# Two steps of VectorE in a kernel of attention and feed-forward: sums of weights put in front of a row's adds, the scaling of x put into the next row

## The chip, the cores and the metric

The kernel runs on one core of a Trainium2 chip. Its time is the device time in microseconds (us), and the number for a kernel is the median of its runs. One execution is taken by the hardware profiler as well; times inside the kernel are from that execution, counted from its first instruction.

The engines are TensorE (PE in the profile; PEld is its loading of weights), VectorE (DVE), ScalarE (ACT), GpSimd (POOL) and SyncE (SP). Each works through its own queue, and semaphores hold an instruction until what it needs is there.

## The reference

Attention for 4 batches of 8 heads, with 768 positions of 64 numbers, and on its result a feed-forward block:

```python
q_bits = (np.einsum('bhsd,dk->bhsk', q, proj) > 0)     # 6 bits: a bucket
mask = q_bucket[:, :, :, None] == k_bucket[:, :, None, :]
scores = np.where(mask, scale * np.matmul(q, k.transpose(0, 1, 3, 2)), -1e9)
attn = softmax(scores)
x = np.matmul(attn, v)        # (B,H,S,D) -> (3072 tokens, 512)
...
g = x @ w_gate                # 512 -> 1536
return (silu(g) * (x @ w_val)) @ w_out
```

All of it is in 32-bit floats.

## The kernel before, in words

**Rows.** The 8 heads of a batch are taken two by two, so there are 16 pairs, numbered n = 0 to 15, four to a batch. Each pair is done in two rows, one for each half of its 768 queries; half 0 comes first. A row has six chunks of 128 keys. The loop at L843 writes one row after the other. For each chunk, `score` (L484) makes the products of q and k for two heads and adds the products of the hash bits into the same bank of PSUM; ScalarE takes the exponential of them into a tile A (L497). `add` (L518) lets VectorE add up the chunks into a tile acc, five instructions (L523, then L527 four times). `attend` (L500) then multiplies A with v (PSUM tile av), and ScalarE copies the result to xT (L516).

**The sums of the softmax.** After the half-1 row's `attend`, `total` (L529) sums acc over its partitions on TensorE (four products into the tile sum, L540), VectorE takes the reciprocal (L548), and eight DMAs of SP spread it over the partitions (L553). The scaling of x is `norm` (L558): one VectorE instruction at L560 multiplies xT of both halves by the spread reciprocals. `total` doesn't write it out but puts it into the list `waiting`, and the main loop decides when the list is emptied (`finish(waiting)`).

**The feed-forward block of a batch** is cut into atoms, which the rows of the next batch take from the list `atoms` behind their attention; a row takes atoms of size 14 (15.75 from pair 8 on), which is one group, or sometimes two. The last batch's atoms run after the last row, one behind the other (L914). Per batch there are six up groups, which make the gate and value products, and then three chunks of the output product (`down_strassen`, tile po). Both use Strassen's scheme: seven products of sums of blocks instead of eight products of blocks. The sums of x are put into the list `first` and written out before the first group.

**An up group** (`both`, L618) is ten atoms in the batches whose scheme is nested (`nested`, all but the first batch). Each atom has one outer product (`outer`, L651), which TensorE makes as fp32 products of 128x384. Two of the outer products, numbered d = 0 and d = 1, are again split into seven products of 128x192 (`deeper`, L694): those are the inner products. They need four sums of weight blocks, which `weigh(d)` (L687) makes on VectorE, 128x128 each, into the tile inner for d = 0 and words for d = 1 (the fourth into the weights' own place in room). Before the change, weigh(0) is written out in atom 1, in front of atom 2, which has the first inner products. All matmuls are written by `product` (L581) and all plain sums by `plus` (L587), so that the profile has them under L584 and L588. After each inner product its bank of PSUM is added into a tile c or hid (L588); three inner products that add into the same bank each have to wait until the one before has been read. At the end of a group `settle` writes out what is left of the gates: L571 multiplies by 1 + tanh, where the tanh is ScalarE's L570, and L575 multiplies gate and value.

**Weights** come by DMAs of GpSimd (`bring`, L322) from DRAM into two places, for every group anew. Each place is filled in three parts, and a part is fetched as soon as the products that used it are done (`free`, L645). Weigh(0) uses the block A12, which is a part by itself.

**Which row has what.** From pair 8 on, a batch's eight rows take: output chunk and up group 0 (half 0); groups 1 to 5, one in each row; then two output chunks, the second in a half-1 row. With pair 8 that is: group 1 in 8's half-1 row, 2 and 3 in pair 9, 4 and 5 in pair 10, output chunks in pair 11, and pair 12 begins with a chunk and the next batch's group 0. So the half-1 rows of pairs 8, 9, 10, 12, 13 and 14 have an up group, and the half-0 rows of pairs 9, 10, 13 and 14.

**The order of the work is written out by hand**: each engine's queue has its instructions in the order in which the program writes them. Before the change the list `waiting` is emptied inside a row's atoms, once atoms of size 11 have been written (L899), so that the scaling of pair n stands in the half-1 row of n, near the end of the group:

```python
            if part >= 11 or u + NCH == N and part >= 6:
                finish(waiting)
```

and weigh(0) stands in the group that uses it:

```python
                    todo[at - 1].insert(0, lambda at, d=d: weigh(d))
```

Of the kernel before, what the change touches and what calls it, by code (L numbers as in the profile page):

```python
# [18 lines left out]
def kernel(  # L19
# [16 lines left out]
    NCH = S // P  # L36
# [3 lines left out]
    NP = H // 2  # L40
# [260 lines left out]
    def scale_ahead():  # L301
        scale_to(min(progress["piece"] + 4, progress["scaled"] + 1))
# [82 lines left out]
    atoms = []  # L385
# [92 lines left out]
    LATE = NP * 2 * NCH  # L478
# [5 lines left out]
    def score(u):  # L484
        n, half, c = units[u]
        qs = slice(half * HQ, (half + 1) * HQ)
        ks = slice(c * P, (c + 1) * P)
        sc = [bank("sc")[:, 0:HQ] for _ in range(2)]
        for x, start in ((T, True), (bits, False)):
            if u < 2 and not start:  # L490
                prepare_pair(1)
            for h in range(2):
                rows = slice(h * D, (h + 1) * D)
                nc.tensor.matmul(sc[h], x["k", n][rows, ks], x["q", n][rows, qs],  # L494
                                 start=start, stop=not start)
        for h in range(2):
            nc.scalar.activation(weights(u)[:, h, 0:HQ], sc[h], AF.Exp,  # L497
                                 scale=SCALE * (OFF / 2 if n <= NP else 1.0))
# [79 lines left out]
    def gate_tile():  # L578
        return ffn.tile([P, HQ], FP32, tag="c", name="c", bufs=5)

    def product(ps, pairs_, start):  # L581

        for i, (a, x) in enumerate(pairs_):
            nc.tensor.matmul(ps, a, x, start=start and i == 0, stop=i == len(pairs_) - 1,  # L584
                             skip_group_check=True)

    def plus(o, a, b, op=ALU.add):  # L587
        nc.vector.tensor_tensor(o, a, b, op=op)  # L588

    def up_strassen(x, b, first):  # L590
# [14 lines left out]
        nested = b > 0  # L605
# [12 lines left out]
        def both(i):  # L618
# [15 lines left out]
            def settle(at):  # L634
                while later and later[0][0] <= at:
                    later.pop(0)[1]()
# [14 lines left out]
            def outer(n, g, at):  # L651
                my = now[g]
                block, to, xs = (
                    (A11, "a", [x[j][:, lo] for j in range(2)]),
                    (S1, "b", [x[j][:, hi] for j in range(2)]),
                    (S2, "a", [t2[:, j] for j in range(2)]),
                    (A12, "c", [x[2 + j][:, lo] for j in range(2)]),
                    (S3, "a", [t3[:, j] for j in range(2)]),
                    (S4, "b", [x[2 + j][:, hi] for j in range(2)]),
                    (A22, "a", [t4[:, j] for j in range(2)]),  # L660
                )[n]
                w = places[g][:, block, :].rearrange("p (j m) -> p j m", m=P)
                if to not in my:
                    my[to] = bank("up")[:, 0:HQ]
                c = my[to]
                product(c, [(w[:, j], xs[j]) for j in range(2)], n in (0, 1, 3))
                spot = ((0, 0), (1, 1), (0, 1), (0, 0), (1, 1), (0, 1), (1, 0))[n]
                copies = (0, 2, 4) if nested else (0, 1, 2)
                if n in copies:
                    nc.scalar.copy(tile_of(g, spot), c)  # L670
                    if n == 4:
                        nc.scalar.copy(tile_of(g, (1, 0)), c)
                elif n < 6:
                    plus(my[spot], my[spot], c)
                    c = my[spot]
                settle(at)
                if n not in copies:
                    finished(g, spot, c, at, 1 if n == 6 else 2)
                free(g, n)
# [3 lines left out]
            def inner_weights(block, rs):  # L683
                vs = [places[g][:, block, j * P : (j + 1) * P] for g in range(2) for j in range(2)]
                return (*vs, *(rs[:, k] for k in range(3)), vs[2])

            def weigh(d):  # L687
                _, block, *_, rs, _ = deep[d]
                v11, v12, v21, v22, r1, r2, r3, r4 = inner_weights(block, rs)
                for o, p, q, op in ((r3, v11, v21, ALU.subtract), (r2, v22, r3, ALU.subtract),  # L690
                                    (r1, r2, v11, ALU.add), (r4, v12, r2, ALU.subtract)):
                    plus(o, p, q, op)
# [29 lines left out]
            todo = [[lambda at, n=n, g=g: outer(n, g, at)] for n in order for g in range(2)]  # L722
            if nested:
                for d, at in ((0, 2), (1, 6)):
                    for go in range(4):
                        todo[at + go].insert(0, lambda at, d=d, go=go: deeper(d, go, at))
                    todo[at - 1].insert(0, lambda at, d=d: weigh(d))

            def step(at):
                if at == 0:  # L730
                    while first:
                        first.pop(0)()
                for do in todo[at]:
                    do(at)
                if at == len(todo) - 1:
                    settle(at + NB)

            for at in range(len(todo)):
                size = 2 if nested and at in (2, 3, 6, 7) else 1
                atoms.append((size, lambda at=at: step(at), at == len(todo) - 1))  # L740

        for i in range(NG // 2):
            both(i)
# [87 lines left out]
    def prepare_pair(count):  # L831
        for _ in range(count):
            rest.extend(f for f in steps.pop(0)() or [] if f)

    def finish(todo):
        while todo:
            todo.pop(0)()

    prepare_pair(4)
    finish(rest)  # L840
    N = len(units)
    credit = 0.0
    for u in range(0, N, NCH):  # L843
        n, half, _ = units[u]
        gating = u >= LATE
        if u == MOVE:
            progress["late"] = True
            for t in late_ring:
                nc.gpsimd.memset(t[:, :, HQ:AW], 1.0)
        for c in range(NCH):  # L850
            score(u + c)
            if u + c == 2 or not gating and half == 1 and c == 2:
                prepare_pair(1)
            if c == 1 and half == 0 and 0 < n <= NP:
                total(n - 1)
            if c:
                add(u + c)
        if half == 1 and n < NP or u == LATE:
            finish(waiting)
        finish(rest)  # L860
        if not gating and half == 0:
            steps = front(n + 1)
        if not gating and half == 0 and u > 0:
            prepare_pair(2)
        for _ in range(1 if u else 2):
            scale_ahead()
        for c in range(NCH):
            attend(u + c)
        if not gating:
            scale_ahead()  # L870
        if half == 1:
            load(n + 2, "qkv" if n + 2 > NP else "v")
        elif not gating:
            prepare_pair(2 if u > 0 else 4)
            if n + 2 <= NP:
                load(n + 2, "qk")
        finish(first)
        prepare_on(0 if u == LATE else 4)
        chores = []
        if half == 1 and n >= NP:  # L880
            total(n)
            if n + 1 < len(pairs):
                chores = [None] + steps.pop(0)()
        prepare_on(0 if LATE - NCH <= u <= LATE else 3 if gating or not half else 1)
        if not gating:
            continue
        if n + 1 < len(pairs) and half == 0:
            steps = front(n + 1)
            chores = [None, steps.pop(0), None, steps.pop(0)]

        credit += 14 if n < 2 * NP else 15.75
        end = True
        part = 0
        while atoms and (credit > 0 or not end):
            size, atom, end = atoms.pop(0)
            credit -= size
            atom()
            part += size
            if part >= 11 or u + NCH == N and part >= 6:  # L899
                finish(waiting)  # L900
                if u + NCH == N:
                    finish([first.pop(0) for _ in range(min(2, len(first)))])
            if 5 < part < 14 if u == LATE else part < (9 if u < LATE + 3 * NCH else 11):
                prepare_on(size)
            if 6 < part < 11 or u == LATE and part > 10:
                scale_ahead()
            for _ in range(size):
                if chores:
                    step = chores.pop(0)
                    chores.extend(step and step() or [])  # L910
        while chores:
            step = chores.pop(0)
            chores.extend(step and step() or [])
# [34 lines left out]
```

The softmax here doesn't subtract the row's maximum and nothing guards it: scores larger than these inputs give would overflow.

## Time and profile before

| | us |
|---|---|
| median of 3 runs | 999.0 (998.54 to 999.03) |
| span of the profiled execution | 997.5 |
| TensorE busy in it | 980.5 (98%) |
| VectorE busy | 671.7 (67%) |
| ScalarE busy | 407.7 (41%) |

The profile is read in this order: the busy time by engine; who waited for whom (a line has engine and source line, the releaser, the total in us, the number of times and the longest); the windows, which give for a stretch of time its length and each engine's busy time in it; and the timeline, in which each line has the start, the length, the engine, the line of the kernel, the operation, the tiles written and read, and how many such instructions are drawn together. An fp32 product is two passes in the profile, so that 34 products of a group are 68 entries.

The chain of work that ended last is nearly all TensorE:

```profile
PE 90%; DVE 6%; issue 2%; ACT 2%; POOL 0%; DMA 0%; DVEq 0%; ACTq 0%; POOLq 0%
```

### The profile page before, as it was taken

Reading aid. Unit: us, or ns where it says so; the run is one execution under the profiler, and the core shown is the slowest. Engines: PE = TensorE matmul, PEld = TensorE weight load, DVE = VectorE, ACT = ScalarE, POOL = GpSimd, SP = SyncE. Lnnn points to the kernel's source line nnn. Section 1 sums busy time; section 2 is a strip of 40 time slices with the busy share of each in tenths; the row PEclk is TensorE's granted clock in tenths of the full one; section 3 lists DMA queues with packets and bytes.
Section 4 is the critical chain, followed back from the end, with each engine's and each line's share of the span. In section 5 each row is a group of like instructions: output and inputs, shape, how many; then the busy total and the mean of one; then the engine's idle time right before and its main releaser. Section 6 shows DMA issues by size and latency. Waiting matters only on the chain.

```text
span 997.5 us, 13575 instructions
## 1 busy us (share of the span) xinstructions
PE 980.5 (98%) x4813; PEld 624.5 (63%) x4813; DVE 671.7 (67%) x1276; ACT 407.7 (41%) x921; POOL 126.9 (13%) x248
## 2 busy tenths in 40 slices
PE   9999999999999999999999999999999999999998
PEld 4444555555577765655566775665656786666687
DVE  5898988888965556777783456776776446667631
ACT  6999555565512233444432313443452202232200
POOL 3222232231100011011010001111110001121000
PEclk9999999999999999999999999999999999999999
DMA  7777685876313043333322114343131102233001
GB/s 233 223 243 227 164 260 174 226 268 154 103 29 75 17 116 92 90 98 78 100 79 58 51 32 111 93 106 92 58 92 33 34 31 90 74 116 101 5 29 36
DMA packets 119987, 107.02 MB, mean 107 GB/s; under 512 B 90032, under 2 KB 104848, under 8 KB 119920
## 3 DMA queue, kind: packets, MB, share of 16 engines
q0 software_dynamic: 18336, 73.29, 22.6%
q1 hardware_dynamic: 100784, 32.67, 14.0%
q8 instruction: 38, 0.62, 0.3%
q10 hardware_dynamic: 800, 0.20, 0.1%
q14 instruction: 29, 0.24, 0.1%
HBM read 81.79 MB, written 17.30 MB: 99 GB/s over the span
## 4 chain that ended last, share of the span: by engine, by line
PE 90%; DVE 6%; issue 2%; ACT 2%; POOL 0%; DMA 0%; DVEq 0%; ACTq 0%; POOLq 0%
PE up L584 40%; PE po L584 21%; PE sc L494 14%; PE av L509 11%; PE sum L540 1%; PE hps L412 1%; DVE hid L575 1%; DVE c L571 1%; DVE hid L588 1%; DVE xT L560 1%; PE tps L396 1%; DVE room L368 0%; DVE inner L588 0%; PE idle L134 0%; DVE acc L527 0%
## 5 line engine op out<-in xcount | busy, mean ns | idle before, releaser
L584 PE MATMUL up<-xT,room 128*128 128x384 f32 (+1 forms) x732 | 243.0, 465 | 0.0
L584 PEld LDWEIGHTS up<-xT,room 128*128 128x128 f32 x732 | 134.8, 190 | 73.3 <-issue 9.8
L584 PE MATMUL up<-xc,room 128*128 128x384 f32 (+1 forms) x540 | 176.8, 455 | 0.0
L327 POOL DMA_DIRECT2D room<-ram x144 | 77.6, 541 | 682.2 <-PE up L584 665.3
L494 PE MATMUL sc<-qT,kT 64*128 64x384 f32 x768 | 160.7, 494 | 0.0
L527 DVE TENSOR_TENSOR acc<-acc,A 128x768 f32<-128x768 f32 x128 | 122.7, 958 | 15.7 <-ACT A L497 2.9
L588 DVE TENSOR_TENSOR c<-c,up 128x192 f32<-128x192 f32 (+1 forms) x198 | 78.9, 406 | 75.2 <-PE up L584 70.9
L584 PEld LDWEIGHTS up<-xc,room 128*128 128x128 f32 x540 | 99.3, 190 | 43.8 <-DVE c L588 1.1
L570 ACT ACTIVATE th<-c 128x384 f32<-128x384 f32 x90 | 47.0, 522 | 162.5 <-DVE c L571 94.5
L497 ACT ACTIVATE A<-sc 128x384 f32<-128x384 f32 x256 | 103.8, 531 | 0.6 <-PE sc L494 0.5
L494 PEld LDWEIGHTS sc<-qT,kT 64*128 64x128 f32 x768 | 69.5, 186 | 52.9 <-issue 39.2
L793 ACT COPY words<-po 128x256 f32<-128x256 f32 x48 | 17.9, 372 | 199.0 <-PE po L584 180.1
L588 DVE TENSOR_TENSOR hid<-hid,up 128x192 f32<-128x192 f32 (+1 forms) x162 | 67.5, 418 | 45.2 <-PE up L584 43.3
L509 PE MATMUL av<-A,vraw 128*64 128x384 f32 (+1 forms) x512 | 88.2, 486 | 0.0
L588 DVE TENSOR_TENSOR words<-words,po 128x256 f32<-128x256 f32 x36 | 15.1, 421 | 102.1 <-PE po L584 102.1
L670 ACT COPY c<-up 128x384 f32<-128x384 f32 x72 | 34.4, 478 | 87.9 <-PE up L584 87.9
L584 PE MATMUL po<-wo,room 128*128 128x256 f32 x288 | 66.6, 380 | 1.5 <-DVE room L588 1.5
L494 PE MATMUL sc<-qb,kb 64*128 64x384 bf16 x384 | 66.7, 323 | 0.5 <-DVE kb L426 0.5
L584 PE MATMUL po<-wo,hid 128*128 128x256 f32 x288 | 66.9, 382 | 0.0
L584 PE MATMUL po<-room,hid 128*128 128x256 f32 x288 | 66.1, 379 | 0.0
L509 PEld LDWEIGHTS av<-A,vraw 128*64 128x64 f32 x512 | 36.7, 137 | 46.0 <-issue 44.1
L584 PEld LDWEIGHTS po<-wo,hid 128*128 128x128 f32 x288 | 54.1, 190 | 12.1 <-issue 4.9
(137 smaller groups left out, 1162.6 us busy)
## 6 DMA issues: line engine op xcount, KB each, us to landing
room<-ram POOLq DMA_DIRECT2D x96, 384.0 KB, 3.7
vraw<-in_v_dram SPq DMA_DIRECT2D x16, 384.0 KB, 3.3
ram<-room POOLq DMA_DIRECT2D x12, 512.0 KB, 5.2
room<-ram POOLq DMA_DIRECT2D x48, 128.0 KB, 3.4
out_dram<-words SPq DMA_DIRECT2D x48, 128.0 KB, 1.7
room<-in_moe_w_out_dram POOLq DMA_DIRECT2D x10, 512.0 KB, 6.6
qraw<-in_q_dram SPq DMA_DIRECT2D x48, 96.0 KB, 3.2
hid<-in_moe_w_gate_dram POOLq DMA_DIRECT2D x9, 512.0 KB, 6.6
```

Of the source, the lines that this page charges most:

```text
L327: nc.gpsimd.dma_start(places[k % 2][:, PARTS[go], :], ram[k % NG][:, PARTS[go], :])
L396: nc.tensor.transpose(ps[:, i * P : (i + 1) * P], raws[name, n][:, half * CH + i, :, :].rearrange("p h d -> p (h d)"), ident)
L412: nc.tensor.matmul(tile_[i * BLOCK : (i + 1) * BLOCK, 0:HQ], hash_w, T[name, n][:, half * HQ : (half + 1) * HQ], start=True, stop=True)
L494: nc.tensor.matmul(sc[h], x["k", n][rows, ks], x["q", n][rows, qs], start=start, stop=not start)
L497: nc.scalar.activation(weights(u)[:, h, 0:HQ], sc[h], AF.Exp, scale=SCALE * (OFF / 2 if n <= NP else 1.0))
L509: nc.tensor.matmul(ps[h * D : (h + 1) * D, 0:width], raws["v", n][:, h, c, :], a[:, h, 0:width], start=c == 0, stop=c == NCH - 1)
L527: nc.vector.tensor_tensor(acc[n, half], acc[n, half], a[:, :, 0:HQ], op=ALU.add)
L570: nc.scalar.activation(th, g, AF.Tanh, scale=0.5)
L584: nc.tensor.matmul(ps, a, x, start=start and i == 0, stop=i == len(pairs_) - 1, skip_group_check=True)
L588: nc.vector.tensor_tensor(o, a, b, op=op)
L670: nc.scalar.copy(tile_of(g, spot), c)
L793: nc.scalar.copy(o, c)
```

## The change

Two steps of VectorE are written out at another place.

- weigh(0) of a nested group goes into a list `ahead` on the group's first atom (`begin.ahead`). `look_ahead` empties that list for the atom that is first in `atoms`. It is called in a group's last atom, ahead of `settle`, and, from pair 8 on, in each row behind the adds. The group's own first step empties the list too, in case nobody did before. weigh(1) stays where it was.
- From pair 8 on, the rows no longer empty `waiting` at size 11. A half-0 row empties it behind its adds, so that the scaling of pair n stands in the half-0 row of n + 1. The last row, and pairs 0 to 7, do as before.

```diff
+    def look_ahead():
+
+        if atoms:
+            finish(getattr(atoms[0][1], "ahead", []))
...
-                    todo[at - 1].insert(0, lambda at, d=d: weigh(d))
+                    if d:
+                        todo[at - 1].insert(0, lambda at, d=d: weigh(d))
+            ahead = [lambda: weigh(0)] if nested else []
 
             def step(at):
                 if at == 0:
                     while first:
                         first.pop(0)()
+                    finish(ahead)
                 for do in todo[at]:
                     do(at)
                 if at == len(todo) - 1:
+                    look_ahead()
                     settle(at + NB)
+
+            def begin():
+                step(0)
+
+            begin.ahead = ahead
 
             for at in range(len(todo)):
                 size = 2 if nested and at in (2, 3, 6, 7) else 1
-                atoms.append((size, lambda at=at: step(at), at == len(todo) - 1))
+                atoms.append((size, (lambda at=at: step(at)) if at else begin, at == len(todo) - 1))
...
-        if half == 1 and n < NP or u == LATE:
+        if n >= 2 * NP:
+            look_ahead()
+        if (n < NP and half == 1) or u == LATE or (n >= 2 * NP and half == 0):
             finish(waiting)
...
-            if part >= 11 or u + NCH == N and part >= 6:
+            if n < 2 * NP and part >= 11 or u + NCH == N and part >= 6:
                 finish(waiting)
```

(`finish` only moves further up in the file.)

More of the change, by code (lines that the diff above doesn't have):

```diff
@@ L579, in gate_tile, with finish @@
         return ffn.tile([P, HQ], FP32, tag="c", name="c", bufs=5)
+    def finish(todo):
+        while todo:
+            todo.pop(0)()
+    def look_ahead():
+        if atoms:
+            finish(getattr(atoms[0][1], "ahead", []))
     def product(ps, pairs_, start):
@@ L833, in prepare_pair @@
             rest.extend(f for f in steps.pop(0)() or [] if f)
-    def finish(todo):
-        while todo:
-            todo.pop(0)()
     prepare_pair(4)
```

## The prediction

> **What bounds the kernel now.** I read the page's first part, then TensorE's waits, then stretches of the timeline around them. The page says that the bound is TensorE, from end to end:
>
> ```profile
> PE 980.5 (98%) x4813; PEld 624.5 (63%) x4813; DVE 671.7 (67%) x1276; ACT 407.7 (41%) x921; POOL 126.9 (13%) x248
> ```
>
> Only time in which TensorE stands still can be won, and an edit that touches no matmul can win no more. In the waits of TensorE (engine, line, releaser: us in total, times, longest) two lines concern the steps that the change moves:
>
> ```profile
> PE up L584 <- DVE inner L588: 5.8, 5, 1.2
> PE up L584 <- DVE hid L588: 4.2, 6, 0.7
> ```
>
> "inner" is weigh(0). Its five waits all lie after the last row, at 848.21, 867.11, 886.01, 904.91 and 923.81, where one group follows the other with no attention between. In the rows weigh(0) holds up nobody. "hid" is six waits, one in each half-1 row of pairs 8, 9, 10, 12, 13 and 14. The windows view (stretch: length, busy time by engine) of a group in a half-1 row and in the half-0 row after it gives their price:
>
> ```profile
> 379.72:398.35 18.63, 17.94 (x72) 11.96 (x69) 12.97 (x32) 7.28 (x15) 2.67 (x5) 1.00 0.38 112
> 407.44:425.12 17.68, 17.68 (x71) 11.98 (x69) 10.74 (x28) 5.71 (x13) 2.67 (x5) 1.00 0.47 106
> ```
>
> The same products take 18.63 us in one and 17.68 us in the other: **0.95 us**, and so in all six (18.63 or 18.64). The timeline (start, us) of the first shows the cause:
>
> ```profile
> 394.39 1.45 PE L584 MATMUL up<-xT,room 128*128 128x384 f32 x4
> ...
> 395.20 1.01 DVE L560 SCALAR_TENSOR_TENSOR xT<-xT,e,acc 128x768 f32<-128x768 f32 x1
> 396.13 0.35 DVE L588 TENSOR_TENSOR hid<-hid,up 128x192 f32<-128x192 f32 x1
> ...
> 396.54 0.59 PE L584 MATMUL up<-words,room 128*128 128x192 f32 x2 [0.69 <-DVE hid L588]
> ```
>
> and of the second, the same place with no scaling of x in it:
>
> ```profile
> 422.09 1.45 PE L584 MATMUL up<-xT,room 128*128 128x384 f32 x4
> 422.90 0.35 DVE L588 TENSOR_TENSOR hid<-hid,up 128x192 f32<-128x192 f32 x1
> 423.38 0.52 PE L584 MATMUL up<-words,room 128*128 128x192 f32 x2
> ```
>
> The last inner product adds into a bank that VectorE must have read first (the hid sum). There that sum starts 0.81 us after the four products (422.09 to 422.90), and TensorE goes on at once, 1.29 us after them. Here the scaling of x, L560, stands in front of it: 395.20 is again 0.81 us after 394.39, but the sum starts at 396.13 and TensorE goes on after 2.15 us.
>
> **What the Trainium skill says.** "TensorE: Matmul & The Clock Gate", section "Architectural detail", has VectorE and ScalarE as strict FIFOs, with matmuls kept in program order: a step in front delays all behind it. The trace agrees (the sum waits out 0.93 us of scaling, 395.20 to 396.13). "Perfetto Trace Analysis", section "Per-instruction lifecycle", says that a matmul's end is estimated, not observed. The trace agrees: four passes are drawn as 1.45 us, yet the next starts 1.29 us after the first. So I take stalls from starts and not from the printed idle time (0.69 for a loss of 0.86).
>
> **The change part by part.** Built, the two programs differ in VectorE's order alone: TensorE, ScalarE, GpSimd and SP have the same instructions in the same order, all DMAs included. No instruction is added or dropped. Ten weigh(0) and seven scalings move.
>
> *The scaling, pairs 8 to 14, from the end of a half-1 row to behind the adds of the next row.* It leaves six stalls behind. Without it the sum starts at 395.20, 0.81 us after the four products, as in the half-0 rows, which don't stall. Gain: 6 x 0.95 = **5.7 us**. The seventh (pair 11) stood among the output products, where TensorE doesn't wait. At its new place it adds 0.93 us of VectorE work. In half-0 rows with a group, VectorE idles 1.97 us before its next sum (408.75 to 410.72), which hides it, with the 0.74 us that come below and the 1.06 that go there. In the rows of pairs 11 and 15 it pushes the parts for the second output product from about 520.65 to 521.6, wanted at 522.27; in pair 12's row, sums that are followed by 2.40 us idle. Cost: nothing.
>
> *A wait moves with it.* In the changed program the first add of acc in a half-0 row (L523) waits for the eight DMAs of the reciprocals (L553), which before held up only the scaling. Queued behind it are the other adds, the scaling and the transposes. Those DMAs are issued from 437.71 on, within 6.10 us, and land in some 2 us (8.8 at most); the add comes some 11 us after the last issue. Cost: nothing.
>
> *weigh(0), ten times, from behind the adds to before the last gates of the group in front.* It is four sums, 1.06 us from the first to the next instruction:
>
> ```profile
> 406.72 0.29 DVE L588 TENSOR_TENSOR inner<-room 128x128 f32<-128x128 f32 x1
> ...
> 407.78 0.97 DVE L457 STREAM_TRANSPOSE qT<-qraw 128x768 f32<-128x768 f32 x1
> ```
>
> It gains nothing: in the rows nobody waited for it, and after the last row, where TensorE does (five times some 1.4 us), its place doesn't change, since `look_ahead` reads the first entry of `atoms` and the loop there takes none out. It costs something. VectorE at the border to a half-1 row:
>
> ```profile
> 426.16 0.55 DVE L575 SCALAR_TENSOR_TENSOR hid<-c,hid 128x384 f32<-128x384 f32 x1
> 426.84 0.56 DVE L571 SCALAR_TENSOR_TENSOR c<-th,c 128x384 f32<-128x384 f32 x1
> 427.31 1.02 DVE L575 SCALAR_TENSOR_TENSOR hid<-c,hid 128x384 f32<-128x384 f32 x2
> 428.36 0.96 DVE L523 SCALAR_TENSOR_TENSOR acc<-room 128x768 f32<-128x768 f32 x1
> 429.42 4.15 DVE L527 TENSOR_TENSOR acc<-acc,A 128x768 f32<-128x768 f32 x4
> ```
>
> The four sums go in after the first line. The first two lines would follow each other by 0.47 us as the others do, so the 1.06 us begin at 426.63 and the next gate at 427.69 instead of 426.84: 0.85 us late. L523 waited 0.11 us for ScalarE, which falls away: the adds start 0.74 us late and end at 433.57 + 0.74 = 434.31. Behind them on TensorE stand the four sums over acc:
>
> ```profile
> 434.18 0.85 PE L540 MATMUL sum<-acc,ones 128*32 128x384 f32 x8
> ```
>
> With 0.06 us for the hand-over (396.48 to 396.54 above) they can start at 434.37: a new stall of **0.19 us**, six times, 1.1 us in all. Behind them wait the hashes and the whole group. No row of this trace has that wait, so I bound it: 0 if the adds catch up, and 0.6 us each (3.6 in all) if the full 1.06 us arrive and restarting costs 0.1 more (after the stop at 396.54 two passes take 0.43 instead of 0.33). I take 0.19. In half-0 rows nothing on TensorE reads acc: nothing.
>
> Does weigh(0) find its blocks? They are among the four transfers issued from 416.40 on within 2.15 us, with a median of 3.4 us to landing: there by about 422, wanted at 426.63.
>
> *Sum*: -5.7 + 1.1 = -4.6 us. The profiled span of 997.5 becomes 992.9. The median of the runs, 999.0, lies 1.5 us above that span, so the time is **994.4 us**.
>
> **The rivals.**
> 1. *No new wait at the sums*: the adds end in time, and only the gain stays: 999.0 - 5.7 = 993.3. For it: acc has 0.61 us to spare now. Against: the arithmetic above misses by 0.19. Chance 0.12.
> 2. *The sums take most of it back* at 0.6 us each: 999.0 - 5.7 + 3.6 = 996.9. For it: VectorE is dense at that border. Against: it has 0.23 us of slack there. Chance 0.08.
> 3. *Slower: weigh(0) waits for its blocks while it holds VectorE's queue.* Place: the border before each of six half-1 rows. It decides once acc comes more than 0.61 - 0.06 + 0.95 = 1.5 us late. If its block came with the group's last transfer (issued 425.49, there at about 429.0), acc would be some 3.2 us late, TensorE 2.7 us: 6 x (2.7 - 0.95) = +10.5, so 1009.5. Against: those blocks are freed and fetched in the middle of the group. Chance 0.04.
> 4. *The change doesn't do what it says*: the hid sum is late for another reason than L560, the six stalls stay and the new ones come: 999.0 + 1.1 = 1000.1. Against: the half-0 rows. Chance 0.04.
>
> **How the numbers follow.** The forecast has 0.72: 994.4. With rivals 1 and 2 it fills the range, 993.3 less 0.3 for the scatter of the runs (998.54 to 999.03) to 996.9: 993.0 to 996.9. Outside lie rivals 3 and 4. I take 0.2% (2 us) as what a measurement of this kernel can tell from no change. Faster, below 997.0: the forecast and rivals 1 and 2, less a little for the end of rival 2, 0.88; slower 0.06 (rival 3, part of 4); same 0.06.
>
> **What would show it.** "PE up <- DVE hid L588" gone from TensorE's waits, and the six windows at about 17.7 us; "PE sum L540 <- DVE acc" new, six times, 0.1 to 0.6 us each; "PE up <- DVE inner L588" unchanged at five times 1.2. Wrong would be: half-1 rows still at 18.6; VectorE's weigh(0) or L523 waiting for a DMA; a stall in a half-0 row.

## The result and the profile after

The changed kernel takes **994.98 us** (median of 4 runs, 994.74 to 995.03) against 999.0 us before, 4.0 us less. The ratio is 0.996, with a 95% interval of 0.9943 to 0.9978. Forecast were 994.4 us in a range of 993.0 to 996.9. In a second series it took 995.0 us beside 998.82 us, with the same ratio (0.9947 to 0.9974); that is the median of the four runs at the full clock, without a fifth whose clock was granted at 0.753 only (1278.52 us), which is also the one that was profiled.

TensorE's waits in the changed kernel, in the same columns as before; L593 and L597 are the lines that were L584 and L588:

```profile
PE up L593 <- DVE inner L597: 5.7, 5, 1.1
PE po L593 <- DVE room L597: 1.5, 2, 1.0
```

The line for hid, 4.2 us in six waits, is gone. The five waits for inner, behind the last row, are as they were. The windows of the same two groups as before, first the one in a half-1 row (stretch, length, then the busy time and number of instructions of PE, PEld, DVE, ACT and POOL, the granted clock, the share and the GB/s of DMA; of all these only the length is used here):

```profile
379.22:396.90 17.68, 17.68 (x71) 11.98 (x69) 11.17 (x27) 7.25 (x15) 2.68 (x5) 1.00 0.35 106
406.00:423.68 17.68, 17.68 (x72) 11.99 (x70) 11.33 (x28) 5.72 (x13) 2.68 (x5) 1.00 0.49 107
```

The two are now equal, where 18.63 stood against 17.68. The timeline of VectorE at the border to a half-1 row shows weigh(0) at its new place:

```profile
424.71 0.55 DVE L575 SCALAR_TENSOR_TENSOR hid<-c,hid 128x384 f32<-128x384 f32 x1
425.18 0.28 DVE L597 TENSOR_TENSOR inner<-room 128x128 f32<-128x128 f32 x1
...
426.24 0.55 DVE L571 SCALAR_TENSOR_TENSOR c<-th,c 128x384 f32<-128x384 f32 x1
426.71 1.02 DVE L575 SCALAR_TENSOR_TENSOR hid<-c,hid 128x384 f32<-128x384 f32 x2
427.64 0.95 DVE L523 SCALAR_TENSOR_TENSOR acc<-room 128x768 f32<-128x768 f32 x1
428.70 4.15 DVE L527 TENSOR_TENSOR acc<-acc,A 128x768 f32<-128x768 f32 x4
```

From the gate to the first add are now 2.93 us (424.71 to 427.64) instead of 2.20 (426.16 to 428.36): acc comes 0.73 us later. What that costs is seen in the window from the first sum over acc (L540) to the group's first product, once in the kernel before and once in this one:

```profile
434.18:435.61 1.43, 1.43 (x18) 0.42 (x17) 0.48 (x1) 0.48 (x1) 0.00 (x0) 1.00 0.15 40
```

```profile
432.73:434.32 1.59, 1.59 (x18) 0.76 (x16) 0.61 (x2) 0.48 (x1) 0.00 (x0) 1.00 0.28 35
```

It is 0.16 us longer, in each of the six rows. The list of waits doesn't show it: the first of the four sums reads the acc of the other half and starts at once, and the time it is drawn with covers the wait of the others. It takes the starts to see it.

One thing was not in the forecast. The scores of a half-0 row, from their first product to the first with v, take 5.05 us, but in the rows of pairs 11 and 15 more. Pair 11 before (first line, with a usual row below it), then after:

```profile
510.14:515.53 5.39, 5.39 (x37) 3.44 (x36) 5.14 (x11) 3.57 (x10) 0.54 (x1) 1.00 0.27 89
454.24:459.29 5.05, 5.05 (x38) 2.69 (x37) 4.69 (x8) 3.88 (x11) 0.54 (x1) 1.00 0.32 106
```

```profile
507.10:512.92 5.82, 5.82 (x37) 3.38 (x37) 5.57 (x11) 3.61 (x11) 0.54 (x1) 1.00 0.43 130
```

There the stall grew from 0.34 to 0.77 us, and by the same amount in pair 15. With that the sum closes: 6 x 0.95 won, less 6 x 0.16 at the sums, less 2 x 0.43 at the scores, is 3.9 us, and the medians differ by 4.0 and 3.8. The spans of the two profiled executions differ by 4.6 (997.5 and 992.9), but 0.66 of that lies ahead of everything that was moved: the scores of pair 8's half-1 row, in front of the first moved step's effect on TensorE, start at 369.23 before and at 368.57 after.

### The profile page after: what moved, and what is told of

Its sections match the earlier page's. It is cut to its first block, busy times and chain, and to the rows that moved or that the text cites. A ratio compares the mean times of both kernels' runs of the same rounds, so it can differ in the third digit from the quotient of the medians.

```text
span 992.9 us, 13575 instructions
## 1 busy us (share of the span) xinstructions
PE 980.0 (99%) x4813; PEld 625.0 (63%) x4813; DVE 670.4 (68%) x1276; ACT 408.1 (41%) x921; POOL 127.3 (13%) x248
## 4 chain that ended last, share of the span: by engine, by line
PE 91%; DVE 5%; issue 2%; ACT 2%; POOL 0%; DMA 0%; DVEq 0%; ACTq 0%; POOLq 0%
PE up L593 41%; PE po L593 21%; PE sc L494 14%; PE av L509 11%; PE sum L540 1%; PE hps L412 1%; DVE c L571 1%; DVE hid L575 1%; PE tps L396 1%; DVE hid L597 1%; DVE room L368 0%; DVE inner L597 0%; PE idle L134 0%; DVE acc L527 0%; ACT th L570 0%
## 5 line engine op out<-in xcount | busy, mean ns | idle before, releaser
L593 PE MATMUL up<-xT,room 128*128 128x384 f32 (+1 forms) x732 | 243.0, 465 | 0.0
L593 PEld LDWEIGHTS up<-xT,room 128*128 128x128 f32 x732 | 134.8, 190 | 73.3 <-issue 9.8
L593 PE MATMUL up<-xc,room 128*128 128x384 f32 (+1 forms) x540 | 176.9, 455 | 0.0
L597 DVE TENSOR_TENSOR c<-c,up 128x192 f32<-128x192 f32 (+1 forms) x198 | 78.9, 406 | 80.9 <-PE up L593 76.5
L593 PEld LDWEIGHTS up<-xc,room 128*128 128x128 f32 x540 | 99.2, 190 | 43.8 <-DVE c L597 1.1
L597 DVE TENSOR_TENSOR hid<-hid,up 128x192 f32<-128x192 f32 (+1 forms) x162 | 67.5, 418 | 43.5 <-PE up L593 41.6
L597 DVE TENSOR_TENSOR words<-words,po 128x256 f32<-128x256 f32 x36 | 15.2, 421 | 99.2 <-PE po L593 99.2
L593 PE MATMUL po<-wo,room 128*128 128x256 f32 x288 | 66.6, 380 | 1.5 <-DVE room L597 1.5
L593 PE MATMUL po<-wo,hid 128*128 128x256 f32 x288 | 66.9, 382 | 0.0
L593 PE MATMUL po<-room,hid 128*128 128x256 f32 x288 | 66.1, 379 | 0.0
L593 PEld LDWEIGHTS po<-wo,hid 128*128 128x128 f32 x288 | 54.1, 190 | 12.1 <-issue 4.9
```

## The experiments

All times are medians, of 4 to 21 runs. Each is compared with the kernel before, run on the same chip: 998.82 us beside the first four (33 runs), 999.17 us beside the last three (7 runs).

**The changed kernel again** (995.0 us, the second series above; its trace is not used, so what is expected of a trace here is read from that of the first series).

> The changed kernel once more, as the measure for the runs beside it. Theory: 995.0 us, 4.0 us below the kernel before. In its trace six windows of the half-1 groups at 17.7 us, six sums 0.16 us longer, and the scores of the half-0 rows of pairs 11 and 15 at 5.82 us instead of 5.40.

**The scaling alone.** The changed kernel with weigh(0) at its old place:

```diff
-                    if d:
-                        todo[at - 1].insert(0, lambda at, d=d: weigh(d))
-            ahead = [lambda: weigh(0)] if nested else []
+                    todo[at - 1].insert(0, lambda at, d=d: weigh(d))
+            ahead = []
```

> The scaling of x moved, weigh(0) where it was before. Theory (the scaling brings all of the gain, weigh(0) ahead only costs, six times 0.16 us at the sums): 1.0 us below the changed kernel, 994.0; the sums at 0.78 us again; the scores of pairs 11 and 15 stay at 5.82. Rival (weigh(0) ahead helps in the rows as well): 995.5 or more. Rival (the longer sums come from the scaling, or from the two together): the same time as the changed kernel, 995.0, and sums still at 0.94 us.

Measured: 994.38 us, ratio to the kernel before 0.9955 (0.9943 to 0.9968). That is 0.6 us below the changed kernel, where 1.0 was expected, and the two intervals overlap, so at that size the times alone say little; the trace says more. The window at the sums, the group behind it, and the scores of pair 11:

```profile
433.61:435.04 1.43, 1.43 (x19) 0.42 (x17) 0.48 (x1) 0.48 (x1) 0.00 (x0) 1.00 0.12 25
507.71:513.52 5.81, 5.81 (x38) 3.38 (x37) 5.56 (x11) 3.61 (x11) 0.54 (x1) 1.00 0.39 128
435.04:452.74 17.70, 17.70 (x72) 11.96 (x69) 12.12 (x31) 7.24 (x15) 2.67 (x5) 1.00 0.37 107
```

The sums are back at 1.43 us, the group keeps its gain (17.70; the missing 0.02 us, in each of the six groups, is all that weigh(0) ahead had brought there), and the scores of pair 11 are as long as in the changed kernel. So the scaling's move brings the gain and the longer scores; weigh(0)'s brings the longer sums.

**weigh(0) alone.** The changed kernel with `waiting` emptied where it was before:

```diff
-        if (n < NP and half == 1) or u == LATE or (n >= 2 * NP and half == 0):
+        if (n < NP and half == 1) or u == LATE:
...
-            if n < 2 * NP and part >= 11 or u + NCH == N and part >= 6:
+            if part >= 11 or u + NCH == N and part >= 6:
```

> weigh(0) moved, the scaling of x where it was before. Theory: six times 0.16 us lost and nothing won, 1.0 us above the kernel before, 1000.0; the half-1 groups stay at 18.6 us; the scores of pairs 11 and 15 stay at 5.40. Rival (weigh(0) ahead takes part in the gain): below 998.5. Rival (VectorE's time is short everywhere, so that any step ahead of the adds costs in full): six times 0.5 us or more, 1002 and up.

Measured: 999.78 us, ratio 1.0009 (1.0000 to 1.0017): 1.0 us above the kernel before, with an interval that reaches down to no difference, so here too the windows decide. They are those at the sums, of the group behind them, and of the scores of pair 11:

```profile
433.59:435.18 1.59, 1.59 (x19) 0.76 (x17) 0.60 (x2) 0.48 (x1) 0.00 (x0) 1.00 0.14 21
435.18:453.79 18.61, 17.92 (x72) 11.99 (x69) 12.01 (x28) 7.28 (x15) 2.67 (x5) 1.00 0.39 111
509.81:515.21 5.40, 5.40 (x38) 3.45 (x37) 5.15 (x11) 3.57 (x10) 0.54 (x1) 1.00 0.32 100
```

The group keeps its stall (18.61, against 18.63 before), the sums have theirs of 0.16, and the scores of pair 11 are as they were. In the rows, weigh(0) ahead costs 0.16 us each time and brings 0.02.

**More sums at the new place.** In the ten moved cases, three of weigh(0)'s four sums are made a second time:

```diff
+            def again():
+                _, block, *_, rs, _ = deep[0]
+                v11, v12, v21, v22, r1, r2, r3, r4 = inner_weights(block, rs)
+                for o, p, q, op in ((r3, v11, v21, ALU.subtract), (r2, v22, r3, ALU.subtract),
+                                    (r1, r2, v11, ALU.add)):
+                    plus(o, p, q, op)
+
             ahead = [lambda: weigh(0)] if nested else []
+            if i and nested and b < B - 1:
+                ahead.insert(0, again)
```

> The changed kernel with three of the four sums of weigh(0) made twice, at the new place, in the ten groups that the change moves (some 0.86 us of VectorE more each; the result stays the same). Theory (the stall is acc's lateness, so above the slack every further us arrives in full at the half-1 sums, and not at all in half-0 rows): six times 0.86, 5.2 us above the changed kernel, 1000.1; the sums 1.0 us later than in the changed kernel at most, the half-0 groups still 17.7 us. Rival (the 0.16 us are a fixed price of a wait on another engine, not of VectorE's time): the same time as the changed kernel within 1 us. Rival (the half-0 rows are at their limit too): ten times 0.86, 1003.6.

Measured: 1000.07 us, ratio 1.0013 (1.0007 to 1.0020): 5.1 us above the changed kernel in the same series, where 5.2 was expected. The wait now has a line of its own, and the window at the sums grew by another 0.85 us while the group behind it is untouched:

```profile
PE sum L540 <- DVE acc L527: 1.1, 6, 0.2
```

```profile
433.88:436.32 2.44, 2.26 (x18) 0.54 (x16) 1.45 (x2) 0.48 (x1) 0.00 (x0) 1.00 0.39 114
436.32:454.00 17.68, 17.68 (x71) 11.99 (x69) 11.17 (x27) 7.25 (x15) 2.67 (x5) 1.00 0.32 94
```

So the stall is acc's lateness beyond its slack: the first 0.73 us of delay cost 0.16, the next 0.86 cost 0.85. It stays six times, and the half-0 rows of pairs 9, 10, 13 and 14, which got the same extra sums, don't stall: their groups still take 17.68 us. The timeline at the sums shows why the line's 1.1 us understate it:

```profile
433.88 0.83 PE L540 MATMUL sum<-acc,ones 128*32 128x384 f32 x2
434.90 0.52 PE L540 MATMUL sum<-acc,ones 128*32 128x384 f32 x3 [0.18 <-DVE acc L527]
```

The first sum goes ahead at 433.88, the others start 1.02 us later, and of that only 0.18 us are outside the drawn length of the first.

**weigh(0) ahead behind the last row too.** The loop there takes the atoms out of the list, so that `look_ahead` finds the next group:

```diff
-    for _, atom, _ in atoms:
-        atom()
+    while atoms:
+        atoms.pop(0)[1]()
```

> The changed kernel, with the atoms behind the last row taken out of the list one by one, so that look_ahead finds the next group's first atom there too. Theory (the five waits of 1.41 us for weigh(0), restart included, lie there and nowhere else): 7.0 us below the changed kernel, 988.0; 'PE up <- DVE inner' gone from TensorE's waits. Rival (behind the last row VectorE is the bound, so that sums put ahead only push the gates back and TensorE waits for a bank instead): less than half of it, 991.5 or more, with a new wait for c or hid.

Measured: 988.04 us, ratio 0.9887 (0.9870 to 0.9903), as expected; the profiled span is 985.9 us, 7.0 below the changed kernel's. VectorE and TensorE at the second of these groups:

```profile
840.64 0.55 DVE L575 SCALAR_TENSOR_TENSOR hid<-c,hid 128x384 f32<-128x384 f32 x1
841.11 0.29 DVE L597 TENSOR_TENSOR inner<-room 128x128 f32<-128x128 f32 x1
...
841.97 0.28 DVE L597 TENSOR_TENSOR room<-room,inner 128x128 f32<-128x128 f32 x1
842.17 0.55 DVE L571 SCALAR_TENSOR_TENSOR c<-th,c 128x384 f32<-128x384 f32 x1
```

```profile
842.41 0.49 PE L593 MATMUL up<-xT,inner 128*128 128x192 f32 x2
```

The sums are ready before the product that wants them, and in this run's waits of TensorE the line for inner is gone, with none for c or hid in its place. In this place the idea behind the edit holds: there is no acc behind it, and TensorE did wait.

**Behind the last row alone.** As in the run above, but in the rows weigh(0) is back at its old place (`if d or b < B - 1`, and `look_ahead` called for the last batch only), with the scaling moved.

> The scaling of x moved; weigh(0) ahead behind the last row alone, in the rows where it was before. Theory: both gains without the stall at the sums, 0.8 us below the run with weigh(0) ahead everywhere (six times 0.14), 987.2. Rival (the sums ahead are worth something in the rows once the end is faster): the same as that run or above.

Measured: 987.06 us, ratio 0.9877 (0.9862 to 0.9892): 1.0 us below the run with weigh(0) ahead everywhere, where 0.8 was expected. In its trace the six stalls of 0.16 us at the sums are gone.

**The gates first.** The same, and for two batches the sums over hid for the output product (`early`) behind the last group's gates:

```diff
-        atoms[at] = (size, lambda: (early(), last()), end)
+        if b in (0, B - 1):
+            atoms[at] = (size, lambda: (early(), last()), end)
+        else:
+            atoms[at] = (size, lambda: (last(), early()), end)
```

> The kernel before this one in the list (weigh(0) ahead behind the last row alone), and in two batches the three sums over hid for the output product put behind the last group's gates instead of in front of them. Theory (the half-0 scores of pairs 11 and 15 take 5.82 us instead of 5.04 because the exponentials stand on ScalarE behind a tanh that waits for a gate behind those three sums): the scores at 5.04 us, twice 0.78, 1.5 us less, 985.7. Rival (the longer scores come from the scaling that now stands in that row, or from something else of VectorE in it): the scores stay at 5.8, the time too. Rival (the sums come too late for the second output product): the scores shorter, but a wait for room at the output product that takes it back.

Measured: 985.48 us, ratio 0.9862 (0.9847 to 0.9876), 1.6 us below the run above, where 1.5 was expected, and the fastest version of this study. The scores of pair 11 and of pair 15:

```profile
506.98:512.02 5.04, 5.04 (x37) 2.69 (x36) 4.78 (x10) 3.92 (x12) 0.54 (x1) 1.00 0.48 150
746.23:751.28 5.05, 5.05 (x38) 2.69 (x37) 4.79 (x10) 3.92 (x12) 0.54 (x1) 1.00 0.47 148
```

They have the length of all others, with the scaling still in those rows, and TensorE's waits have no new line at the output products. So it is not the scaling's new place that holds the scores, but the three sums in front of the gates. Why the stall grew when the scaling left the row in front is read from the timelines of VectorE and ScalarE there, before and after:

```profile
508.18 0.55 DVE L588 TENSOR_TENSOR c<-c,up 128x384 f32<-128x384 f32 x1
...
511.96 0.52 ACT L570 ACTIVATE th<-c 128x384 f32<-128x384 f32 x1 [2.20 <-DVE c L571]
512.39 1.62 ACT L497 ACTIVATE room<-sc 128x384 f32<-128x384 f32 x4
```

```profile
505.56 0.56 DVE L597 TENSOR_TENSOR c<-c,up 128x384 f32<-128x384 f32 x1 [0.33 <-PE up L593]
...
509.35 0.52 ACT L570 ACTIVATE th<-c 128x384 f32<-128x384 f32 x1 [2.21 <-DVE c L571]
509.78 1.62 ACT L497 ACTIVATE room<-sc 128x384 f32<-128x384 f32 x4
```

The exponentials stand behind a tanh that waits for a gate of VectorE, which stands behind the three sums. Before, they began 2.25 us after the first score (510.14 to 512.39); after, 2.68 us (507.10 to 509.78). What differs lies ahead of the three sums. Before, VectorE did its last addition into c at 508.18, 1.96 us ahead of the first score, right behind the hid sum that TensorE was waiting for; after, it does it at 505.56, 1.54 us ahead, and has idled for 0.33 us there until TensorE had made the product. While TensorE stood still, VectorE had caught up by some 0.4 us; without that stall it comes to the border with so much more still to do. (This catching up is read from the two traces and is not shown by a run of its own: in every run here that keeps the three sums in front of the gates, the scores take 5.40 us where TensorE stood still for the hid sum and 5.82 where it did not.)

## Why the prediction was right

**What bounds the kernel** held: all that was won or lost is time in which TensorE stood still, and no matmul became faster.

**The scaling** was the gain, of the size forecast for the groups: six half-1 groups from 18.63 to 17.68 us, 5.7 us together. The run with the scaling alone keeps it (17.70), the one with weigh(0) alone has 0.02 us of it (18.61). Rival 4, in which something else held the hid sum, falls with that.

**The moved wait** cost nothing, as said: in the changed kernel's trace VectorE's L523 never waits for a DMA.

**weigh(0) in the rows** gained next to nothing (0.02 us a group) and cost 6 x 0.16 us, where 0.19 was forecast; acc was 0.73 us late, against 0.74. The kernel with more sums shows the slack from the other side. Rival 1, no new wait, and rival 2, 0.6 us each, both fall. (The 0.23 us of slack given under rival 2 don't fit the forecast's own sum, where 1.06 us of work make acc 0.74 late, so 0.32.) So does rival 3: weigh(0) followed the gate in front of it by 0.47 us (424.71 to 425.18), and the waits of VectorE have no line for its blocks.

**weigh(0) behind the last row** stayed without effect, as read from the code; the kernel that takes the atoms out shows what was left there, 7.0 us (five times 1.4).

**What was off** is a term that the sum set to nothing: "Cost: nothing" for the scaling's move. For the rows of pairs 11 and 15 the forecast asked whether the parts for the second output product come in time, and they do (no wait there is new). It did not look at the scores ahead of them. It took 6 x 0.95 as the whole gain "as in the half-0 rows", and did not ask what the time that TensorE stood still had been worth to VectorE. In two of the six rows 0.43 us were lost again at the scores that follow, 0.9 us in all: the other terms give 4.7 us together, and 3.9 are left. By the prediction's own list "a stall in a half-0 row" was a sign of being wrong, and these two are such stalls.

The time came out 0.6 us above the forecast. It lies inside the range, but the upper end of that range was made for longer sums over acc; that it held this loss as well is luck. So is the span of the changed kernel, 992.9 us, which is the forecast to the digit: the profiled execution of the kernel before took 999.45 us, 0.45 above the median that was set against its span, and that span has 0.66 us more than the changed kernel's ahead of the first moved step. The gain of the change itself is 3.9 us, where 4.6 were forecast.

A new line among the waits was a bad sign to name for the sums at this size: 0.16 us show in the starts alone.

It wasn't tried whether the last stall of TensorE ahead of the final output products (1.0 us, the wait for room) can be taken away as well.

## What to carry to other kernels

- When one engine is busy throughout, price a move of another engine's step by what stands behind it in that engine's queue at its old place and at its new one, and by who waits for that; the step's own length is only the bound.
- A stall that is taken away may also have been time in which other engines caught up. Look at the next place where they are late: part of the gain can be lost again there (here, as the traces read, 0.9 of 5.7 us).
- A look ahead in a list is only as good as the list's upkeep: here the one stretch in which it paid off (7.0 us) was the one in which nobody took the entries out.

## What the runs showed that was not expected

- A wait of TensorE of 0.16 us left no line in the waits and no idle time in the trace, and one of 1.0 us at the sums was listed as 0.18 each, where a product drawn in front of it covered the rest.
- A stall of 0.95 us that every one of six rows had was worth 0.95 us in four of them and 0.52 us in two.
